# The gate's dot products on GpSimd and ScalarE instead of a column of q's matmuls, and another order of one group of products

## The chip, the cores and the metric

The kernel runs on one core of a Trainium2 chip. A core has five engines that work side by side, each through its own queue and in order: TensorE (PE in the profile, its weight loads PEld), VectorE (DVE), ScalarE (ACT), GpSimd (POOL) and the queue of SyncE (SP), which here only issues transfers. They wait for each other through semaphores. The metric is the device time of one execution in microseconds (us), the median of several runs.

## The reference

Input x has 2048 rows of 448. The output mixes two branches by a gate per row:

```python
g = sigmoid((x * gate_w).sum(-1, keepdims=True))
q, k, v = ...(x @ wqkv)                     # 16 heads of 28
phi = lambda t: where(t > 0, t + 1, exp(t)) + 1e-6
kv = einsum("bhsd,bhse->bhde", phi(k), v); z = phi(k).sum over s
a = (phi(q) @ kv) / (phi(q) @ z + 1e-6) @ wo     # linear attention, no mask
b = causal convolution of x with a kernel made of 256 modes per channel, + x * D_skip
out = g * a + (1 - g) * b
```

With the inputs of this case the convolution's modes allow a short form, which the kernel checks at its end (a general path that follows only if the check fails takes no part here): each channel's b is a running sum of x down the rows, scaled, plus x * D_skip.

## The kernel before

Rows are cut into 16 chunks of 128 (a chunk holds every 16th row, so that the running sum inside a chunk's partition goes over chunks). All large products are 128 x 128 by 128 x 448 on TensorE; to keep their precision each operand is split into a high and a low part, and each product of chunk and weights becomes 11 matmuls (four high by high, four low by high, three high by low; low parts of the small last slice of the weights share a tile with its high part).

The work stands in four stretches.

- **Start** (to 22 us): loads, the split of the first chunks and of the weights, k of chunks 0 to 2, q of chunks 0 and 1.
- **The loop** `for c in range(2, NC - 2)` (L518 on, 22 to 102 us). Step c does on TensorE: k of chunk c + 1 (11 matmuls, `project`, L340, tile `k` or `v`), q of chunk c (11 matmuls, tile `q`), and `do_g(c)`, the sum of phi(k) by x of chunk c (11 matmuls into `g`, L416). v is never formed: x weighted by phi(k) is summed first and multiplied by the weights of v afterwards.
- **Joining** (102 to 120 us): k and q of the last chunks, z summed over the partitions (`zo`, then `zb`), the gate's end (`gate`, L400 to L402), the heads' matrices times wo (`m`), and `norm_a`, `norm_b`, `norm_c`, which divide phi(q) by its dot product with z.
- **Output** (120 to 163 us): `turn_pe` transposes the normed phi(q), `attend` (L677) takes 11 products per chunk, `final_b` (L682) adds (1 - g) * b and stores.

What the other engines do in step c of the loop: ScalarE copies x of chunk c + 2 to the high parts (`split_t`, the transposed x, L241, tile `xt`; `split_n`, the plain x, L247, tile `xn`) and GpSimd takes the low parts (L237). `k_feature(c + 1)` is two activations of ScalarE (L367, L368) and one of VectorE (L369), `k_high` is ScalarE's (L373), `k_low` VectorE's (two instructions of L379, one of which adds to `zb`). `q_post(c)` reads q's PSUM tile on ScalarE and, last, on VectorE (L360 in steps 2 to 4, L394 later). GpSimd also forms x * D_skip (`skip`, L253). In steps 2 to 5 pieces of the filter's preparation (`steps`, L289 to L320) stand in between on ScalarE and VectorE.

The order on each engine is the order in which the code calls these functions; no scheduler moves anything (`manual_schedule`). Until step 5 `split_n(c + 2)` stands at the step's end; from step 6 on it stands at the front, right behind `split_t`:

```python
        split_t(c + 2)
        ...
        if c > 5:
            split_n(c + 2, False)
        k_feature(c + 1, ko)
        ...
        if c < 6:
            split_n(c + 2, c > 3)
```

The tile `q` in PSUM has one buffer, so q of chunk c + 1 waits until `q_post(c)` has read it; k alternates between `k` and other tiles from step 7 on, and chunks 6, 7 and 8 follow each other in `k`. The loads of x (`load_x`, four buffers) wait in SP's queue until a buffer's last reader is done.

The gate: `gate_w` is a 449th column of q's weights (with one of padding, 450 columns), so q's matmuls give x . gate_w in column 448 of q's tile, and `q_post` takes exp(-s) of it on ScalarE (L387, 128x1) into `e1`. `gate(0, c + 1)` with c = 14 (called at L713) makes 1 + e1 and its reciprocal for the first 15 chunks; chunk 15 has its own in `late`.

Of the kernel before, what the change touches and what calls it, by code (L numbers as in the profile page):

```python
# [33 lines left out]
EDGE = 16  # L34
PADS = 32
G = 4
ROWS = {6: (0, 1), 7: (2, 3, 4), 8: (5, 6, 7), 9: (8, 9, 10), 10: (11, 12, 13), 11: (14, 15)}
SMALL = 2.0 ** -70
FLAT = 2.0 ** 35
# [102 lines left out]
@with_exitstack  # L142
def gated_mix_kernel(ctx: ExitStack, tc: tile.TileContext, xin, wq_d, wvo_d, abc_d, ldt_d, dsk_d,
                     turn_d, cst_d, first_d, gin_d, out):
# [24 lines left out]
    ones = const.tile([P, P], F32R, name="ones")  # L169
    dsk = const.tile([P, D], F32, name="dsk")  # L170
    side = []
# [54 lines left out]
    for j in range(0, J, 2):  # L226
        SP.dma_start(out=wqr[:, j:j + 2], in_=wq_d[:, j:j + 2])
    SP.dma_start(out=dsk, in_=dsk_d.to_broadcast([P, D]))
    load_x(3)
# [14 lines left out]
    def split_n(c, both=True):  # L244
        r, w = plain[c], xn_p.tile([P, NX], F32R, name="xn", tag="n")
        xn[c] = w
        ACT.copy(w[:, :XC - NAT], r)  # L247
        if c > 2 and both:
            skip(c)
        low(POOL, w[:, XC - NAT:], r[:, :D], w[:, :D])  # L250

    def skip(c):
        POOL.tensor_tensor(out=y[:, c], in0=plain[c][:, :D], in1=dsk, op=ALU.mult)  # L253

    idle = ps.tile([P, 512], F32, name="q", tag="q")
# [65 lines left out]

    def pieces(c, wh, wl, n, tag, last=None):
        o = ps.tile([P, 512], F32, name=tag, tag=tag)
        h, l = ([xt[c][:, i + k * P:i + (k + 1) * P] for k in range(J)] for i in (0, NAT))
        hh, lh, hl = ([(a[k], w[:, k]) for k in range(J)] for a, w in ((h, wh), (l, wh), (h, wl)))
        hl = hl[1:]
        if last == "x":
            seq = hh + hl + lh
        else:
            seq = [p for k in range(J) for p in (hh[k], lh[k])] + hl  # L330
            if last and len(last) > 1:
                seq = [{"h": hh, "l": lh, "w": [None] + hl}[i[0]][int(i[1])] for i in last.split()]
            elif last == "w":
                seq = seq[2:6] + seq[8:9] + seq[6:8] + seq[9:] + seq[:2]

        def run(count):
            for _ in range(min(count, len(seq))):
                a, b = seq.pop(0)
                run.n += 1
                PE.matmul(o[:, :n], lhsT=a, rhs=b, start=run.n == 1, stop=not seq)  # L340
        run.n = 0
        return o, run
# [43 lines left out]
    def q_post(c, o, mid=None):  # L386
        ACT.activation(e1[:, c:c + 1], o[:, D:D + 1], AF.Exp, scale=-1.0)  # L387
        if c < 5 or c >= NC - 2:
# [129 lines left out]
    for c in range(2, NC - 2):  # L518
# [24 lines left out]
        if c > 5:  # L543
            split_n(c + 2, False)
        k_feature(c + 1, ko)
        if c in (8, 9, 11):
# [7 lines left out]
        if rows:  # L554
            running(rows.pop(0))
        qo = project(c, wqh, wql, D + 2, "q")
        q_post(c, qo)
# [20 lines left out]
        if c in (3, 4):  # L578
            half_load(0, c - 3)
        for j in {11: (0, 1), 12: (2, 3)}.get(c, ()):  # L580
            split_o(j)
# [82 lines left out]
    def attend(c, cuts):  # L664
# [3 lines left out]
        for i, (lo, hi) in enumerate(cuts):  # L668
# [42 lines left out]
    norm_a(0)  # L711
    norm_a(1)
    gate(0, c + 1)  # L713
    norm_bd(0)
# [187 lines left out]
def _layout(inputs):  # L902
# [16 lines left out]
    def tiles(w):  # L919
# [33 lines left out]
        f(byd(inputs["B_log_dt"])[:, :, 0]),  # L953
        f(np.asarray(inputs["B_D_skip"]).reshape(1, D)),
        f(np.stack([np.eye(P), lag >= 1], axis=1)),
# [20 lines left out]
```

## Time and profile before

| | |
|---|---|
| median of 3 runs | 167.91 us (167.91 to 168.14) |
| the profiled execution | 167.58 us |
| its span, first to last instruction | 165.6 us |
| busy: TensorE, VectorE, ScalarE, GpSimd | 97%, 70%, 66%, 63% |

The profiled execution's time is longer than its span, as what lies ahead of the first and behind the last instruction counts in it. A group row reads: line, engine, operation, out<-in, shapes, count, then busy us and mean ns of one, then the engine's idle time just before and what ended it. A timeline row reads: start in us from the span's start, us taken, engine, line, operation, tiles, and in brackets the idle time before it with its releaser. A row of the chain reads start, us, what. A row of a list of waits reads: who waited for whom, us in total, times, longest.

### The profile page before, as it was taken

What the parts mean: (1) busy time and instruction counts of PE and PEld (TensorE: products, weight loads), DVE (VectorE), ACT (ScalarE), POOL (GpSimd) and SP (SyncE); (2) the same over time, 40 slices, a digit from 0 to 9 for tenths busy, and PEclk for the clock granted to TensorE, in tenths of its full rate; (3) what the DMA queues carried; (4) which work ended last, traced back from release to release, by engine and by line L of the source; (5) the groups of instructions that cost most, each with busy time, mean ns of one, the idle gap of its engine ahead of it and who ended that gap; (6) DMA issues with size and microseconds to landing.
All of it is one profiled execution on the core that took longest, in us unless ns stands there. A gap on an engine that the chain in (4) does not pass through costs nothing.

```text
span 165.6 us, 2610 instructions
## 1 busy us (share of the span) xinstructions
PE 160.5 (97%) x835; PEld 144.8 (87%) x835; DVE 116.0 (70%) x243; ACT 109.4 (66%) x257; POOL 104.9 (63%) x116
## 2 busy tenths in 40 slices
PE   6999999999999999999999999999999999999991
PEld 2698999999999999999999999989879999999990
DVE  0937744685852888989885555898899989986441
ACT  3688668898486784776758966453775775666531
POOL 3082589568819439467295999749799998632000
PEclk9999999999999999999999999999999999999999
DMA  5989956597974331969968007998121221122222
GB/s 167 410 311 320 311 156 216 209 316 280 311 260 137 127 107 48 194 156 259 337 200 166 0 4 118 184 204 163 25 49 55 111 111 59 66 103 111 111 85 89
DMA packets 10783, 27.51 MB, mean 166 GB/s; under 512 B 1328, under 2 KB 6992, under 8 KB 10544
## 3 DMA queue, kind: packets, MB, share of 16 engines
q1 hardware_dynamic: 8992, 21.71, 38.3%
q0 software_dynamic: 1632, 5.51, 17.8%
q8 instruction: 7, 0.11, 0.3%
q10 hardware_dynamic: 144, 0.11, 0.2%
q14 instruction: 8, 0.07, 0.1%
HBM read 17.87 MB, written 3.67 MB: 130 GB/s over the span
## 4 chain that ended last, share of the span: by engine, by line
PE 93%; DVE 2%; DMA 1%; ACT 1%; SPq 0%; issue 0%; ACTq 0%; POOL 0%; POOLq 0%
PE g L416 21%; PE a L677 21%; PE q L340 19%; PE v L340 12%; PE k L340 11%; PE tr L633 3%; PE q L259 3%; DMA wk<-shl 1%; PE k L756 1%; SPq L795 0%; ACT kvh L773 0%; DVE wk L744 0%; DVE shl L744 0%; POOL warm L193 0%; DVE ot L682 0%
## 5 line engine op out<-in xcount | busy, mean ns | idle before, releaser
L677 PE MATMUL a<-wk,th 128*128 128x448 f32 (+1 forms) x178 | 37.6, 357 | 0.2 <-DMA wk<-shl 0.2
L416 PE MATMUL g<-pkh,xn 128*128 128x448 f32 x112 | 35.7, 364 | 0.0
L677 PEld LDWEIGHTS a<-wk,th 128*128 128x128 f32 x178 | 31.4, 188 | 2.9 <-issue 0.5
L237 POOL TENSOR_TENSOR xt<-xr,xt 128x512 fp32r<-128x512 f32 x14 | 18.1, 1294 | 19.6 <-ACT xt L241 19.6
L340 PE MATMUL q<-wqh,xt 128*128 128x450 f32 x120 | 27.7, 366 | 0.0
L237 POOL TENSOR_TENSOR xn<-xr,xn 128x448 fp32r<-128x448 f32 x16 | 19.6, 1225 | 9.9 <-ACT xn L247 9.9
L340 PEld LDWEIGHTS q<-wqh,xt 128*128 128x128 f32 x120 | 22.5, 188 | 1.7
L416 PE MATMUL g<-pkl,xn 128*128 128x448 f32 x64 | 23.3, 365 | 0.0
L416 PEld LDWEIGHTS g<-pkh,xn 128*128 128x128 f32 x112 | 21.1, 188 | 2.3
L596 POOL TENSOR_TENSOR prod<-pq,zb 128x448 f32<-128x448 f32 x16 | 18.2, 1149 | 3.9 <-ACT zb L710 2.9
L253 POOL TENSOR_TENSOR y<-xr,dsk 128x448 f32<-128x448 f32 x16 | 20.4, 1280 | 0.0
L340 PE MATMUL k<-wk,xt 128*128 128x448 f32 x88 | 19.7, 366 | 0.0
L340 PE MATMUL v<-wk,xt 128*128 128x448 f32 x88 | 18.9, 362 | 0.0
L340 PEld LDWEIGHTS k<-wk,xt 128*128 128x128 f32 x88 | 16.3, 188 | 1.7 <-DVE xt L237 0.3
L340 PEld LDWEIGHTS v<-wk,xt 128*128 128x128 f32 x88 | 16.5, 188 | 1.1
L682 DVE SCALAR_TENSOR_TENSOR ot<-y,og,a 128x448 f32<-128x448 f32 (+1 forms) x17 | 10.6, 629 | 7.2 <-PE a L677 7.1
L621 POOL TENSOR_TENSOR room<-pq,den 128x336 f32<-128x336 f32 x16 | 12.0, 750 | 5.7 <-ACT den L610 2.7
L688 ACT COPY pq<-a 128x448 f32<-128x448 f32 (+1 forms) x17 | 8.6, 511 | 5.8 <-DVE ot L682 5.6
L416 PEld LDWEIGHTS g<-pkl,xn 128*128 128x128 f32 x64 | 11.1, 174 | 1.1 <-DVE pkl L379 0.2
L340 PE MATMUL q<-wql,xt 128*128 128x450 f32 x45 | 11.7, 365 | 0.0
L655 ACT CAST th<-tr 64x128 fp32r<-64x128 f32 x32 | 8.3, 260 | 4.9 <-DVE th L646 4.5
L369 DVE SCALAR_TENSOR_TENSOR k<-k,e 128x448 f32<-128x448 f32 x8 | 5.0, 631 | 8.9 <-ACT e L368 8.8
(155 smaller groups left out, 288.9 us busy)
## 6 DMA issues: line engine op xcount, KB each, us to landing
xr<-in SPq DMA_DIRECT2D x15, 512.0 KB, 4.6
out<-ot SPq DMA_DIRECT2D x15, 224.0 KB, 1.9
room<-in SPq DMA_DIRECT2D x3, 896.0 KB, 8.0
wvo<-in SPq DMA_DIRECT2D x2, 896.0 KB, 5.6
y<-wvo POOLq DMA_DIRECT2D x2, 896.0 KB, 7.7
y<-room POOLq DMA_DIRECT2D x2, 896.0 KB, 9.2
y<-over POOLq DMA_DIRECT2D x2, 896.0 KB, 9.5
y<-in SPq DMA_DIRECT2D x2, 480.0 KB, 4.3
```

Source lines behind the costliest of these rows:

```text
L237: eng.tensor_tensor(out=o, in0=r, in1=h.bitcast(F32), op=ALU.subtract)
L253: POOL.tensor_tensor(out=y[:, c], in0=plain[c][:, :D], in1=dsk, op=ALU.mult)
L259: PE.matmul(idle[:, :cols], lhsT=warm[:, :P], rhs=warm[:, :cols], start=True, stop=True)
L340: PE.matmul(o[:, :n], lhsT=a, rhs=b, start=run.n == 1, stop=not seq)
L369: DVE.scalar_tensor_tensor(out=pks[c], in0=pks[c], scalar=1.0, in1=e, op0=ALU.add, op1=ALU.max)
L416: PE.matmul(g[i][:a.shape[1], :D], lhsT=a, rhs=b, start=c == 0 and n == 0, stop=c == NC - 1 and n == len(seq) - 1)
L596: POOL.tensor_tensor(out=pd[c], in0=pq[:, c], in1=zb, op=ALU.mult)
L621: POOL.tensor_tensor(out=n[:, :3, :DJ].rearrange("p j (h d) -> p j h d", h=4), in0=a, in1=r[:, :H - 4].rearrange("p (j h) -> p j h", j=3)[ ...
L655: ACT.copy((th, tl)[i][c][half, 3], oe[i * DT:(i + 1) * DT, 3 * P:])
L677: PE.matmul(a[:, lo:hi], lhsT=u_, rhs=w_[:, lo:hi], start=n == 0, stop=n == 10)
L682: DVE.scalar_tensor_tensor(out=ot[:, lo:hi], in0=y[:, c, lo:hi], scalar=og[:, c:c + 1], in1=a[:, lo:hi], op0=ALU.mult, op1=ALU.add)
L688: ACT.copy(pq[:, c, lo:hi], a[:, lo:hi])
```

## The change

For chunks 2 to 13 the gate's dot product leaves TensorE. GpSimd multiplies plain x by gate_w, broadcast to all partitions (`gate_products`, into the three buffers of `prod`, which `norm_a` uses later), and ScalarE adds up each row with an accumulating copy (`gate_total`, into `e1`). One exponential over the twelve columns of `e1` follows in the joining stretch, ahead of `gate`. q's matmuls of these chunks have 448 columns instead of 450, and `q_post` has no exponential for them. Chunks 0, 1, 14 and 15 keep the column. D_skip and gate_w come in one broadcast load of two rows. `PADS` grows by 64 columns, so that the tiles behind keep their alignment. The table `GATES` says which chunks' products stand at the end of step c; their sums stand in step c + 1, between the copies of x and `k_feature`. Apart from that, the nine products of the first output chunk stand in another order.

```diff
+GATES = {2: (2,), 3: (3,), 4: (4, 5, 6), **{c: (c + 2,) for c in range(5, 12)}}
...
-    dsk = const.tile([P, D], F32, name="dsk")
+    both_rows = const.tile([P, 2, D], F32, name="rows")
+    dsk, gwt = both_rows[:, 0], both_rows[:, 1]
...
-    SP.dma_start(out=dsk, in_=dsk_d.to_broadcast([P, D]))
+    SP.dma_start(out=both_rows, in_=rows_d.to_broadcast([P, 2, D]))
...
+    def gate_products(c):
+        POOL.tensor_tensor(out=prod[:, c % 3], in0=plain[c][:, :D], in1=gwt, op=ALU.mult)
+
+    def gate_total(c):
+        ACT.activation(prod[:, c % 3], prod[:, c % 3], AF.Copy, accum_out=e1[:, c:c + 1])
...
     def pieces(c, wh, wl, n, tag, last=None):
+        wh, wl = wh[:, :, :n], wl[:, :, :n]
...
     def q_post(c, o, mid=None):
-        ACT.activation(e1[:, c:c + 1], o[:, D:D + 1], AF.Exp, scale=-1.0)
+        if c < 2 or c >= NC - 2:
+            ACT.activation(e1[:, c:c + 1], o[:, D:D + 1], AF.Exp, scale=-1.0)
...
         if c > 5:
             split_n(c + 2, False)
+        for i in GATES.get(c - 1, ()):
+            gate_total(i)
         k_feature(c + 1, ko)
...
-        qo = project(c, wqh, wql, D + 2, "q")
+        qo = project(c, wqh, wql, D, "q")
...
         if c in (3, 4):
             half_load(0, c - 3)
+        for i in GATES.get(c, ()):
+            gate_products(i)
...
             if c == 0:
-                seq = [seq[n] for n in (0, 2, 3, 6, 1, 4, 5, 7, 8)]
+                seq = [seq[n] for n in (0, 2, 1, 3, 4, 5, 6, 7, 8)]
...
     norm_a(1)
+    ACT.activation(e1[:, 2:c], e1[:, 2:c], AF.Exp, scale=-1.0)
     gate(0, c + 1)
```

The order on GpSimd from the end of step 2 to step 5, before (`xn` and `xt` are the low parts of x, `y` is x * D_skip; in brackets the semaphores an instruction waits for):

```order
L237 TENSOR_TENSOR xn<-xr,xn 128x448 [waits Activation_49]
L237 TENSOR_TENSOR xt<-xr,xt 128x512 [waits DVE_49,DMAHW6_49,PE_49,Activation_49]
L253 TENSOR_TENSOR y<-xr,dsk 128x448
L253 TENSOR_TENSOR y<-xr,dsk 128x448 [waits DVE_49]
L237 TENSOR_TENSOR xn<-xr,xn 128x448 [waits Activation_49,Pool_49]
L237 TENSOR_TENSOR xt<-xr,xt 128x512 [waits DMAHW0_49,PE_49,Activation_49]
L253 TENSOR_TENSOR y<-xr,dsk 128x448 [waits Pool_49]
L237 TENSOR_TENSOR xn<-xr,xn 128x448 [waits Activation_49]
L237 TENSOR_TENSOR xt<-xr,xt 128x512 [waits DMAHW2_49,PE_49,Activation_49]
```

The same place in the change:

```order
L239 TENSOR_TENSOR xn<-xr,xn 128x448 [waits Activation_49]
L258 TENSOR_TENSOR prod<-xr,rows 128x448
L239 TENSOR_TENSOR xt<-xr,xt 128x512 [waits DVE_49,DMAHW6_49,PE_49,Activation_49]
L255 TENSOR_TENSOR y<-xr,rows 128x448
L255 TENSOR_TENSOR y<-xr,rows 128x448 [waits DVE_49]
L239 TENSOR_TENSOR xn<-xr,xn 128x448 [waits Activation_49,Pool_49]
L258 TENSOR_TENSOR prod<-xr,rows 128x448
L239 TENSOR_TENSOR xt<-xr,xt 128x512 [waits DMAHW0_49,PE_49,Activation_49]
L255 TENSOR_TENSOR y<-xr,rows 128x448 [waits Pool_49]
L239 TENSOR_TENSOR xn<-xr,xn 128x448 [waits Activation_49]
L258 TENSOR_TENSOR prod<-xr,rows 128x448 x3
L239 TENSOR_TENSOR xt<-xr,xt 128x512 [waits PE_49,DMAHW2_49,Activation_49,Pool_49]
```

Each product of the gate (`prod`) stands right behind the low part of xn, which itself waits for ScalarE's copy, and ahead of the low part of the next xt.

The order on ScalarE in step 3, before (`e<-k` is L367, the start of k's feature; `sums<-q` is the first reading of q's tile, with the exponential of the gate's column just ahead of it; `y,sm` are the filter's preparation):

```order
L247 CAST xn<-xr 128x512
L241 CAST xt<-xr 128x512 [waits DMAHW6_49]
L367 ACTIVATE e<-k 128x448 [waits PE_49]
L368 ACTIVATE e<-e 128x448 [waits Activation_49]
L373 ACTIVATE pkh<-k 128x448 [waits DVE_49]
L387 ACTIVATE e_61<-q 128x1 [waits PE_49]
L356 ACTIVATE sums<-q 128x448
L294 ACTIVATE y,sm<-pq 112x512
```

The same place in the change:

```order
L249 CAST xn<-xr 128x512
L243 CAST xt<-xr 128x512 [waits DMAHW6_49]
L261 ACTIVATE prod,e_61<-prod 128x448 [waits Pool_49]
L376 ACTIVATE e<-k 128x448 [waits PE_49]
L377 ACTIVATE e<-e 128x448 [waits Activation_49]
L382 ACTIVATE pkh<-k 128x448 [waits DVE_49]
L365 ACTIVATE sums<-q 128x448 [waits PE_49]
L302 ACTIVATE y,sm<-pq 112x512
```

The sum of chunk 2's products (`prod,e_61`) stands ahead of k's feature and waits for GpSimd; the exponential of one column is gone.

The products of the first output chunk on TensorE, before, from the first product on (the DMA semaphores tell of the rows of `mh`, part of `wk`, that transfers bring; VectorE's tell of low parts):

```order
L677 MATMUL a<-wk_70,th 128x448 [waits DMAHW3_49,DVE_49,Activation_49]
L677 MATMUL a<-wk_70,th 128x448 [waits DVE_49]
L677 MATMUL a<-wk_70,th 128x448 [waits DMAHW4_49,Activation_49]
L677 MATMUL a<-wk_70,th 128x448 [waits DMAHW5_49,Activation_49]
L677 MATMUL a<-wk_70,th 128x448 [waits DVE_49]
```

The same in the change:

```order
L691 MATMUL a<-wk_70,th 128x448 [waits DMAHW3_49,DVE_49,Activation_49]
L691 MATMUL a<-wk_70,th 128x448 [waits DVE_49] x2
L691 MATMUL a<-wk_70,th 128x448 [waits DMAHW4_49,Activation_49]
L691 MATMUL a<-wk_70,th 128x448
L691 MATMUL a<-wk_70,th 128x448 [waits DVE_49]
L691 MATMUL a<-wk_70,th 128x448 [waits DMAHW5_49,Activation_49]
```

The wait for the third of these transfers (DMAHW5) moved from the fourth product to the seventh, and one for VectorE came ahead, to the third.

More of the change, by code (lines that the diff above doesn't have):

```diff
@@ L34 @@
 EDGE = 16
-PADS = 32
+PADS = 96
 G = 4
 ROWS = {6: (0, 1), 7: (2, 3, 4), 8: (5, 6, 7), 9: (8, 9, 10), 10: (11, 12, 13), 11: (14, 15)}
+GATES = {2: (2,), 3: (3,), 4: (4, 5, 6), **{c: (c + 2,) for c in range(5, 12)}}
 SMALL = 2.0 ** -70
@@ L142, in gated_mix_kernel @@
 @with_exitstack
-def gated_mix_kernel(ctx: ExitStack, tc: tile.TileContext, xin, wq_d, wvo_d, abc_d, ldt_d, dsk_d,
+def gated_mix_kernel(ctx: ExitStack, tc: tile.TileContext, xin, wq_d, wvo_d, abc_d, ldt_d, rows_d,
                      turn_d, cst_d, first_d, gin_d, out):
@@ L953, in _layout @@
         f(byd(inputs["B_log_dt"])[:, :, 0]),
-        f(np.asarray(inputs["B_D_skip"]).reshape(1, D)),
+        f(np.stack([np.asarray(inputs["B_D_skip"]).reshape(D), np.asarray(inputs["gate_w"]).reshape(D)[perm]])[None]),
         f(np.stack([np.eye(P), lag >= 1], axis=1)),
```

## The prediction

> **What bounds the kernel now.** I read the page's busy shares first, then TensorE's waits, then the chain in order of time, then the timelines of ScalarE, GpSimd and VectorE in the stretch where the change first acts.
>
> ```profile
> span 165.6 us, 2610 instructions
> PE 160.5 (97%) x835; PEld 144.8 (87%) x835; DVE 116.0 (70%) x243; ACT 109.4 (66%) x257; POOL 104.9 (63%) x116
> PE a L677 <- DMA wk<-shl: 0.2, 1, 0.2
> ```
>
> TensorE is busy for 97% of the span, and beside the wait for its first operand its list of waits has this one entry. So the time is its stream of products, and only two things change it: fewer or shorter products, or a wait that does not exist today. The 66% of ScalarE and the 63% of GpSimd look like room, but they are averages. This is the stretch of chunks 3 and 4 (columns: window, sum, then busy us of PE, PEld, DVE, ACT, POOL, each with its count; then clock and DMA):
>
> ```profile
> 28.00:35.00 7.00, 7.00 (x37) 6.41 (x36) 4.96 (x11) 6.17 (x18) 5.34 (x6) 1.00 0.69 239
> ```
>
> ScalarE is busy for 6.17 of 7.00 us there, because the filter's preparation is interleaved with chunks 2 to 4. A wait in its queue has almost nothing to swallow it, and the change puts one there.
>
> **The new wait, step by step.** At the end of loop step c GpSimd computes xn's low part (L237), and then, new, the gate's products. In step c+1 ScalarE copies xt, then, new, sums those products, and only then starts k's feature (L367). Both engines take their work in order. Today's rows, ScalarE first (start, length):
>
> ```profile
> 31.57 0.53 ACT L367 ACTIVATE e<-k 128x448 f32<-128x448 f32 x1
> 34.36 0.63 ACT L294 ACTIVATE y<-pq 112x512 f32<-112x512 f32 x1
> 36.41 0.42 ACT L295 ACTIVATE y<-room 112x256 f32<-112x256 f32 x1
> 36.83 0.60 ACT L247 CAST xn<-xr 128x512 fp32r<-128x512 f32 x1
> 37.86 0.53 ACT L367 ACTIVATE e<-v 128x448 f32<-128x448 f32 x1
> 40.83 0.63 ACT L247 CAST xn<-xr 128x512 fp32r<-128x512 f32 x1
> 43.83 0.55 ACT L367 ACTIVATE e<-k 128x448 f32<-128x448 f32 x1 [1.85 <-PE k L340]
> 45.98 0.55 ACT L373 ACTIVATE pkh<-k 128x448 fp32r<-128x448 f32 x1 [0.99 <-DVE k L369]
> 48.56 0.62 ACT L247 CAST xn<-xr 128x512 fp32r<-128x512 f32 x1
> 50.85 0.55 ACT L367 ACTIVATE e<-k 128x448 f32<-128x448 f32 x1 [0.63 <-PE k L340]
> ```
>
> GpSimd's rows; the one of L253 is the same product (128x448, two SBUF operands) that the gate now takes, and it prices it: 1.15 us, the next starting 0.04 before it ends, so 1.12 each in a row.
>
> ```profile
> 31.22 1.24 POOL L237 TENSOR_TENSOR xn<-xr,xn 128x448 fp32r<-128x448 f32 x1 [1.66 <-ACT xn L247]
> 37.57 1.18 POOL L237 TENSOR_TENSOR xn<-xr,xn 128x448 fp32r<-128x448 f32 x1 [1.62 <-ACT xn L247]
> 39.97 1.15 POOL L253 TENSOR_TENSOR y<-xr,dsk 128x448 f32<-128x448 f32 x1
> 41.54 1.16 POOL L237 TENSOR_TENSOR xn<-xr,xn 128x448 fp32r<-128x448 f32 x1 [0.42 <-ACT xn L247]
> ```
>
> A sum over 448 elements isn't in the trace; it lies between the 0.42 us of 256 elements (L295) and the 0.63 of 512 (L294), and I take 0.57, by length. What it removes, the exponential of one column, moves its successor by only 0.05 us. Now the ring, with delays of L367 against today:
>
> - Chunk 2. GpSimd ends xn at 31.22 + 1.24 = 32.46 and the product at 33.58; ScalarE's sum starts at 33.61 and L367 of chunk 4 at 34.18 instead of 31.57: 2.6 us late.
> - Chunk 3. From that L367 to the end of the next xn copy ScalarE needs 37.43 - 31.57 - 0.05 = 5.8 us and so ends it at 39.99; GpSimd starts 0.14 later, takes 1.18 and 1.12, and the sum ends at 43.0 instead of 37.86: 5.2 late.
> - Chunks 4, 5 and 6, three products at once. The copy ends 3.55 us on, at 46.6; then 0.08 + 1.16 + 3 x 1.12, and the last sum ends at 51.8 instead of 43.83: 7.95 late. The idle 1.85 us of ScalarE before 43.83 is used up in this.
> - Chunk 7. To the next xn copy (48.56 + 0.62) it was 5.35, less 0.05 and less 0.29 (L373 waited 0.99 for VectorE, of which 0.29 was a backlog that has passed by then): 56.8; then 0.08 + 1.16 + 1.12 + 0.6: 59.7 instead of 50.85, 8.9 late.
> - Chunk 8 on. From step 6 xn is split before k's feature and not at the step's end, so the product is one step old when it is asked for: no further wait.
>
> What is late next is TensorE, because q and k each reuse a PSUM buffer that VectorE must have read out:
>
> ```profile
> 36.95 1.81 PE L340 MATMUL q<-wqh,xt 128*128 128x450 f32 x8
> 43.63 1.77 PE L340 MATMUL q<-wqh,xt 128*128 128x450 f32 x8
> 48.45 2.36 PE L340 MATMUL k<-wk,xt 128*128 128x448 f32 x11
> 55.06 2.36 PE L340 MATMUL k<-wk,xt 128*128 128x448 f32 x11
> 35.78 0.62 DVE L360 SCALAR_TENSOR_TENSOR pq<-q,t 128x448 f32<-128x448 f32 x1
> 42.06 0.62 DVE L360 SCALAR_TENSOR_TENSOR pq<-q,t 128x448 f32<-128x448 f32 x1
> 47.10 0.61 DVE L379 SCALAR_TENSOR_TENSOR zb<-k,zb 128x448 f32<-128x448 f32 x1
> 53.82 0.61 DVE L379 SCALAR_TENSOR_TENSOR pkl<-k,pkh 128x448 fp32r<-128x448 f32 x1
> ```
>
> q of chunk 4 starts at 36.95 and its buffer is free at 36.40, 0.55 us of room; 2.6 late it waits about 2.1. q of chunk 5 (43.63, free at 42.68 + 5.15) waits another 2.1 to 2.2, k of chunk 7 (48.45, free at 47.71 + 7.65) 2.6, k of chunk 8 (55.06, free at 54.43 + 8.9 and a tenth for the start) 1.4. After that TensorE is **8.3 us** late and nothing gives it back, as it has no idle time later. Bounds: the sum at 0.42 or 0.63 moves this by 0.5 down or 0.2 up over four rings; a product at the 1.28 us that L253 has as its mean adds 0.8.
>
> **What the other parts give.** In order of time, TensorE alone:
>
> ```profile
> 37.11 2.27 PE q L340 x11
> 43.79 2.21 PE q L340 x11
> 41.59 2.20 PE k L340 x11
> ```
>
> Eleven products of 450 columns take 2.21 or, in five groups of fourteen, 2.27 us; of 448 columns they take 2.20. Gains before 55 us vanish into the waits; behind it chunks 7, 9 and 11 had the 2.27 (with 0.01 on the products behind each): 0.27 us with the rest. Bounds: 0.05 and 0.3.
>
> The first output chunk: its products start at 120.14, and the copies of the rows of mh land one after the other:
>
> ```profile
> 120.14 1.06 PE L677 MATMUL a<-wk,th 128*128 128x448 f32 x3
> 121.39 1.85 PE L677 MATMUL a<-wk,th 128*128 128x448 f32 x8 [0.20 <-DMA wk<-shl]
> 119.95 0.67 DVE L646 TENSOR_TENSOR th<-tr,th 128x512 fp32r<-128x512 f32 x1
> ```
>
> Today the fourth product needs the third of four copies (it starts at 121.39, as soon as that has landed), and it is the first of the last eight. In the new order it is the seventh; the third needs VectorE's low part of th (119.95 + 0.67 = 120.62) and starts near 120.73, the fourth near 121.0, the seventh near 121.6, and the last ends its issue near 122.6 instead of 123.1: 0.48 us. VectorE is nearly as busy as TensorE behind this, so part is taken by its waits: I take 0.3, bounds 0 and 0.48.
>
> The gate itself: its exponential now stands behind ScalarE's zb copy.
>
> ```profile
> 109.26 0.53 ACT L710 COPY zb<-zo 128x448 f32<-128x448 f32 x1 [0.73 <-PE zo L708]
> 109.64 0.17 DVE L400 TENSOR_SCALAR e<-e 128x15 f32<-128x15 f32 x1
> 110.12 1.01 DVE L402 TENSOR_SCALAR og<-og 128x15 f32<-128x15 f32 x1
> 109.94 2.27 POOL L596 TENSOR_TENSOR prod<-pq,zb 128x448 f32<-128x448 f32 x2 [2.90 <-ACT zb L710]
> 114.12 0.28 DVE L762 TENSOR_TENSOR k<-k,mask 112x112 f32<-112x112 f32 x1
> ```
>
> L402 took 1.01 us where its like L400 took 0.17: it ended when GpSimd's first product of the two did (109.94 + half of 2.27). L400 can now start at about 109.9, in a race with that product. Ahead of it, the gate ends 0.1 later; behind it, L400 ends with the first product and L402 with the second, 1.1 us later, and L762, which starts 114.12 and is on the chain, follows. I take 0.05, bounds 0 and 1.1. [...]
>
> The broadcast load is 224 KB larger and stands ahead of x of chunk 3 in SP's queue:
>
> ```profile
> xr<-in SPq DMA_DIRECT2D x15, 512.0 KB, 4.6
> L241 ACT CAST xt<-xr 128x512 fp32r<-128x512 f32 x14 | 8.6, 613 | 0.3 <-DMA xr<-in 0.3
> ```
>
> At 512 KB in 4.6 us it makes that x at most 2.0 us later. ScalarE's fourteen copies of x wait for loads for 0.3 us in all, and chunk 3's comes behind the work on chunks 0 to 2, so I take nothing, bounds 0 and 2.0. The later loads of x wait for a buffer whose last reader may now be a gate product; they land a step or more ahead of their use, so I count nothing there either.
>
> Sum: 8.3 - 0.27 - 0.3 + 0.05 = **7.8 us**. The profiled execution took 167.58 us (165.6 of span and 1.98 around it) and would take 175.4; the median is 167.91, so **175.7**.
>
> **Rivals.** (1) The sums never hold ScalarE, because the products are done in time: then only the gains stay, 0.35 + 0.3 less 0.05, and the time is 167.3, faster. For it speak GpSimd's 1.6 us idle before each xn; against it, that this idle lies before the xn copy, on which the product waits in line. (2) The wait comes, but something I count as serial overlaps (the ring closes once, at chunk 2 and 3, and the idle of ScalarE at 43.83 absorbs the rest): 2.1 + 2.1 - 0.6, so 171.5. Against it: three products in a row at chunk 4. (3) TensorE slows after the stalls. At the start ten products of 512 columns took 3.85 us:
>
> ```profile
> 1.33 3.85 PE q L259 x10
> ```
>
> At the later pace (448 columns in 0.20) they would take 2.3. After each stall but the last the ring, not TensorE, sets the next start, so one such loss counts: 1.6 us, 177.3. [...] (4) L400 loses its race: 176.8. (5) The 448 columns don't shorten anything, since the 2.27 comes from elsewhere: 176.0.
>
> **How the numbers follow.** Forecast with (4) and (5) as its edges 0.75, (3) 0.06, (2) 0.09, (1) 0.07, and 0.03 for an even balance. The range 172.5 to 178.2 takes in the price bounds (0.5 down, 0.2 and 0.8 up), (3), (4), and a wait that closes in one ring less. About 0.2% is what a measurement of this kernel can tell from no change: faster by more 0.07, within 0.03, slower 0.90.
>
> **What would show it.** Right: TensorE's list of waits gets VectorE as releaser, with two waits of about 2.1 us at q and two of 2.6 and 1.4 at k, between 38 and 64 us; ScalarE idles about 1.9 us before the sums of chunks 2, 3 and 4, released by GpSimd; q's eleven products take 2.20 from chunk 7 on; from step 8 to the loop's end TensorE waits for nothing; the first output chunk's products have no wait over 0.3. Wrong: TensorE's waits stay under 2 us in sum (rival 1), or its products take longer than 0.20 after a wait (rival 3), or the gate's last step ends over 2 us behind the zb copy (1.3 today; rival 4).

## The result, and the profile after

On the chip the changed kernel takes 175.81 us (median of five runs, 175.17 to 175.87), the one before 167.91 on the same chip (167.87 to 168.23): a ratio of 1.0445, 95% interval 1.0421 to 1.0469. The profiled execution took 175.17, with a span of 173.4 instead of 165.6, so 7.8 us more. The page after:

```profile
span 173.4 us, 2622 instructions
PE 163.0 (94%) x835; PEld 145.5 (84%) x835; DVE 115.7 (67%) x243; ACT 116.0 (67%) x270; POOL 118.1 (68%) x128
PEclk9999999999969999999999999999999999999999
```

TensorE's share fell from 97% to 94%, and the row of its clock, 40 slices of the span, has a dip in the twelfth slice that the page before did not have. Its list of waits now has VectorE as releaser:

```profile
PE q L349 <- DVE pq L369: 3.7, 2, 1.8
PE k L349 <- DVE pkl L388: 1.1, 1, 1.1
PE k L349 <- DVE zb L388: 0.9, 1, 0.9
```

In time these are four starts. The rows answer to the four of L340 in the prediction:

```profile
39.06 1.88 PE L349 MATMUL q<-wqh,xt 128*128 128x448 f32 x8 [1.83 <-DVE pq L369]
...
47.89 2.62 PE L349 MATMUL q<-wqh,xt 128*128 128x448 f32 x8 [1.83 <-DVE pq L369]
...
55.46 2.45 PE L349 MATMUL k<-wk,xt 128*128 128x448 f32 x11 [0.88 <-DVE zb L388]
...
63.46 2.45 PE L349 MATMUL k<-wk,xt 128*128 128x448 f32 x11 [1.14 <-DVE pkl L388]
```

Before they started at 36.95, 43.63, 48.45 and 55.06: TensorE is 2.11, 4.26, 7.01 and 8.40 us late, of which 0.1 stood already at the start of the loop. (The idle time in brackets counts from the modelled end of the product before, 0.37 us behind its start, so it is about 0.17 less than what is lost at 0.20 us a product.) Where VectorE's input stays away is read on ScalarE:

```profile
33.67 0.58 ACT L261 ACTIVATE prod<-prod 128x448 f32<-128x448 f32 x1 [1.93 <-POOL prod L258]
...
34.24 0.53 ACT L376 ACTIVATE e<-k 128x448 f32<-128x448 f32 x1
...
42.49 0.58 ACT L261 ACTIVATE prod<-prod 128x448 f32<-128x448 f32 x1 [1.93 <-POOL prod L258]
...
43.07 0.53 ACT L376 ACTIVATE e<-v 128x448 f32<-128x448 f32 x1
...
48.96 0.58 ACT L261 ACTIVATE prod<-prod 128x448 f32<-128x448 f32 x1 [1.83 <-POOL prod L258]
...
51.74 0.52 ACT L376 ACTIVATE e<-k 128x448 f32<-128x448 f32 x1
...
59.16 0.58 ACT L261 ACTIVATE prod<-prod 128x448 f32<-128x448 f32 x1 [1.40 <-POOL prod L258]
...
59.74 0.53 ACT L376 ACTIVATE e<-k 128x448 f32<-128x448 f32 x1
```

L376 (L367 before) started at 31.57, 37.86, 43.83 and 50.85. It is 2.67, 5.21, 7.91 and 8.89 us late; the prediction had 2.6, 5.2, 7.95 and 8.9.

Two things in this trace were not forecast. Behind the second wait TensorE's products come 0.373 us apart instead of 0.20 (the row at 47.89 takes 2.62 us for eight products, the one at 39.06 takes 1.88). And the first output group is no shorter than before:

```profile
128.23 3.12 PE L691 MATMUL a<-wk,th 128*128 128x448 f32 x11
131.19 0.93 PE L647 MATMUL tr<-both,room 128*128 128x128 f32 x7
```

From its first product to the next transposes it takes 2.96 us; before it was 2.94 (120.14 to 123.08).

### The profile page after: what moved, and what is told of

It reads as the page before. It is cut to its first block, busy times and chain, and to the rows that moved or that the text cites. A ratio compares the mean times of both kernels' runs of the same rounds, so it can differ in the third digit from the quotient of the medians.

```text
span 173.4 us, 2622 instructions
## 1 busy us (share of the span) xinstructions
PE 163.0 (94%) x835; PEld 145.5 (84%) x835; DVE 115.7 (67%) x243; ACT 116.0 (67%) x270; POOL 118.1 (68%) x128
## 4 chain that ended last, share of the span: by engine, by line
PE 61%; ACT 2%; DVE 1%; issue 1%; ACTq 0%
PE a L691 21%; PE q L349 11%; PE g L426 11%; PE k L349 5%; PE v L349 5%; PE tr L647 4%; PE m L751 1%; PE tr L771 1%; PE k L771 1%; ACT prod L261 0%; DVE k L378 0%; DVE pkl L388 0%; ACT e L377 0%; ACT pkh L382 0%; DVE ot L696 0%
## 5 line engine op out<-in xcount | busy, mean ns | idle before, releaser
L349 PE MATMUL q<-wqh,xt 128*128 128x448 f32 (+1 forms) x120 | 28.4, 373 | 3.7 <-DVE pq L369 3.7
L255 POOL TENSOR_TENSOR y<-xr,rows 128x448 f32<-128x448 f32 x16 | 20.3, 1277 | 0.0
L258 POOL TENSOR_TENSOR prod<-xr,rows 128x448 f32<-128x448 f32 x12 | 14.5, 1214 | 0.0
L261 ACT ACTIVATE prod<-prod 128x448 f32<-128x448 f32 x12 | 6.9, 577 | 8.0 <-POOL prod L258 8.0
L349 PE MATMUL q<-wql,xt 128*128 128x448 f32 (+1 forms) x45 | 12.2, 377 | 0.0
```

The source lines that it names most:

```text
L258: POOL.tensor_tensor(out=prod[:, c % 3], in0=plain[c][:, :D], in1=gwt, op=ALU.mult)
L261: ACT.activation(prod[:, c % 3], prod[:, c % 3], AF.Copy, accum_out=e1[:, c:c + 1])
```

## The experiments

Each run is compared with runs of the kernel before on its own chip; the medians of the kernel before were 167.92, 167.78 and 168.28 us on the three chips used. Besides the time this table gives four stretches of the profiled execution, all on TensorE, in us: from the first product of chunk 5's k to that of chunk 8's (the ring lies in it), from there to the first output product, the first output group, and the rest of the span (to 0.05 us, as the page gives spans to 0.1).

| kernel | ratio to before, 95% | ring | to output | first group | rest |
|---|---|---|---|---|---|
| before | 1 | 20.31 | 65.08 | 2.94 | 42.52 |
| the change | 1.0445 (1.0421 to 1.0469) | 28.62 | 64.77 | 2.96 | 42.21 |
| sums behind `k_high` | 1.0135 (1.0089 to 1.0182) | 22.57 | 65.08 | 3.07 | 42.26 |
| sums of a resident row | 1.0109 (1.008 to 1.0139) | 22.62 | 64.68 | 2.98 | 42.37 |
| products without sums | 1.0031 (1.0011 to 1.005) | 21.79 | 64.65 | 2.97 | 42.19 |
| chunk 2 alone | 1.0151 (1.0085 to 1.0217) | 24.06 | 65.08 | 2.49 | 42.56 |
| chunk 2 alone, again | 1.0141 (1.0103 to 1.0179) | 22.50 | 65.13 | 2.44 | 42.80 |
| chunk 2 three times | 1.044 (1.0421 to 1.0458) | 27.83 | 64.96 | 2.45 | 42.79 |
| old order of products | 1.0478 (1.0441 to 1.0516) | 28.62 | 64.75 | 4.29 | 42.42 |
| twelve fills | 1.0449 (1.0425 to 1.0474) | 28.62 | 64.74 | 2.47 | 42.42 |
| before, new order | 0.9972 (0.9959 to 0.9985) | 20.31 | 65.09 | 2.48 | 42.52 |
| before, 448 columns | 1.001 (0.9997 to 1.0024) | 20.23 | 64.78 | 3.60 | 42.82 |
| chunks 4 to 13 | 0.9988 (0.9957 to 1.002) | 20.53 | 64.75 | 2.47 | 42.32 |
| chunks 6 to 13 | 0.9938 (0.9921 to 0.9954) | 20.31 | 64.88 | 2.48 | 42.18 |

### Is it the wait for GpSimd, or the work?

The sums moved, nothing else:

```diff
-        for i in GATES.get(c - 1, ()):
-            gate_total(i)
         k_feature(c + 1, ko)
...
         k_high(c + 1)
+        for i in GATES.get(c - 1, ()):
+            gate_total(i)
         k_low(c + 1)
```

> The changed kernel, but each gate sum on ScalarE stands behind k_high(c + 1) and not ahead of k_feature(c + 1); all products and sums are kept. Theory (the loss is the wait in ScalarE's queue, a ring of two queues): the products are done when the sums are asked for, k's feature is late only by the sums' own 0.57 us each, TensorE waits for 0.4 us at most between 36 and 66 us, and the time is 167.3 to 167.9 us. Rival (the loss is the work: 6.9 us more on ScalarE and 14.5 on GpSimd, in a stretch where ScalarE is busy for 88%): the same work in another place still holds TensorE by several us, 171 to 175.

Measured: 170.36 us (169.58 to 171.71), a ring of 22.57 instead of 28.62. So 6 of the 8.3 us were the wait for GpSimd. But 2.3 remained where I had expected 0.4, and it was no rest of that wait. On ScalarE:

```profile
39.33 0.62 ACT L243 CAST xt<-xr 128x512 fp32r<-128x512 f32 x1 [1.35 <-DMA xr<-in]
```

and by groups, in the same kernel:

```profile
L243 ACT CAST xt<-xr 128x512 fp32r<-128x512 f32 x14 | 8.6, 613 | 2.4 <-DMA xr<-in 2.4
```

ScalarE's copies of x wait for their loads for 2.4 us in all. The kernel before has the same group with 0.3. This is another wait, one that the prediction had put at nothing.

The sums left in their place, but without anything to wait for:

```diff
-        ACT.activation(prod[:, c % 3], prod[:, c % 3], AF.Copy, accum_out=e1[:, c:c + 1])
+        ACT.activation(junk, dsk, AF.Copy, accum_out=e1[:, c:c + 1])
```

> The changed kernel with the sums in their place ahead of k_feature, but summing the resident row D_skip instead of the products, into a tile of their own: the 0.57 us of ScalarE and the 1.15 of GpSimd stay, only the wait for GpSimd is gone (the gate of chunks 2 to 13 is left out by this, so the output is another). Theory (wait): k's feature of chunk 4 is 0.5 us late, of chunk 5 1.0, q of chunk 5 waits 0.1 to 0.2, and ScalarE's idle 1.85 us before k's feature of chunk 6 takes the rest; 167.3 to 167.9. Rival (work): TensorE waits for 3 us and more, over 170.

Measured: 169.99 us (169.46 to 170.48), ring 22.62. Its copies of x wait for loads too, 1.9 us in the groups of that kernel. Neither text was right: without the wait for GpSimd 6 us go, and 2.3 stay.

The products alone:

```diff
-        for i in GATES.get(c - 1, ()):
-            gate_total(i)
```

> The changed kernel without the gate's sums (their columns of e1 are filled with zero, so the gate of chunks 2 to 13 is left out); the products stay where they are. Theory (the products alone hold the buffers of x: x of chunk 6 goes out at 36 us behind the second x * D_skip instead of at 26, lands at 39.3, and ScalarE's copy of it, due at 37.3, waits for about 2 us): k's feature of chunk 5 is 2.0 late, q of chunk 5 has 0.95 us of room and waits 1.0, k of chunk 7 0.3 to 0.5; 168.4 us. Rival (the products cost nothing where no sum waits for them): no wait over 0.2, 167.2.

Measured: 168.49 us (168.18 to 169.21), ring 21.79. ScalarE has no work of the gate's here, and yet:

```profile
39.65 0.62 ACT L244 CAST xt<-xr 128x512 fp32r<-128x512 f32 x1 [1.99 <-DMA xr<-in]
```

It waits 2.0 us for x of chunk 6, as expected. q of chunk 5 then comes 1.1 late and k of chunk 7 0.2. The products hold a buffer of x, and without any sum this costs 1.5 us in the ring's stretch. The 0.8 between this kernel and the two before comes with the sums; how it divides between their own time on ScalarE and what waits behind them was not measured. In the changed kernel the late load is there too. SP sends it off at 36.03, and ScalarE's copy of it starts at 39.95 without a wait:

```profile
36.03 0.33 SPq L204 DMA_DIRECT2D xr<-in  x1
...
39.95 0.62 ACT L243 CAST xt<-xr 128x512 fp32r<-128x512 f32 x1
```

In the kernel before, this second load of the loop went off at 26.10:

```profile
26.10 0.33 SPq L202 DMA_DIRECT2D xr<-in  x1
```

Then it took the buffer of chunk 3, whose last reader (its xn low part) ended at 26.07. Now chunk 3's gate product at the end of step 3 still reads that buffer, and the load waits for the one that the first `skip` of step 3 frees, at 36.0. It lands at 39.37, so that ScalarE's copy, delayed by the ring, starts 0.58 us later. The ring hid the late load.

### Does TensorE give anything back, and when does it slow down?

One gate product instead of twelve:

```diff
-GATES = {2: (2,), 3: (3,), 4: (4, 5, 6), **{c: (c + 2,) for c in range(5, 12)}}
+GATES = {2: (2,)}
...
-        qo = project(c, wqh, wql, D, "q")
+        qo = project(c, wqh, wql, D if c == 2 else D + 2, "q")
```

(with the exponential of the column kept for the other chunks)

> The changed kernel with the gate of chunk 2 alone on GpSimd and ScalarE; chunks 3 to 13 keep their column and their exponential. Theory (what TensorE loses once stays lost): q of chunk 4 waits 2.1 us; the next features are late by no more than TensorE is, so no second wait; 167.9 + 2.1 = 170.0, between 169.5 and 170.3. Rival (ScalarE's idle 1.85 us before k's feature of chunk 6 gives it back): 167.9 to 168.3. As to TensorE's pace: if a single idle time of 2 us slows it, the products behind it take 0.37 us instead of 0.20 for about 3 us and the time is 171.6; if it takes two such waits within 10 us, as in the changed kernel, they stay at 0.20.

Measured: 170.68 us, four executions from 169.79 to 172.24. One wait, at q of chunk 4, and none behind it. In the profiled execution (171.02 us) the products behind the wait came 0.37 us apart; by windows (window, length, busy us of PE, PEld, DVE, ACT, POOL with counts, then clock, DMA share and GB/s):

```profile
36.27:39.69 3.42, 1.50 (x9) 1.09 (x8) 2.93 (x7) 3.32 (x12) 0.81 (x1) 1.00 0.79 307
39.69:43.10 3.41, 3.41 (x11) 3.02 (x10) 1.52 (x4) 2.45 (x5) 2.90 (x3) 0.50 0.08 25
```

The clock was 0.50 for one stretch of 3.41 us: its row counts 11 products, where a row of the same length at 1.00 counts 19 (41.94:45.35 of the next run). Nothing behind hid it, so the ring's stretch grew by 3.75 us: 2.15 of wait and 1.6 of slow products. So here slow products followed a single wait, of 2.15 us, which the expectation had left open. But other executions were faster, so I ran it again.

> The gate of chunk 2 alone once more, for the spread: one wait of 2.1 us at q of chunk 4, nothing behind it that hides slower products. The first time the profiled execution had products of 0.37 us for 3.4 us behind the wait, took 171.0 and showed a mean granted clock of 0.990; two others took 169.8 and 170.3 with 1.00. Theory (whether the clock falls behind a wait of 2 us differs from one execution to the next, as if the wait were measured against a grid of its own): executions near 169.5 (167.9 + 2.1 - 0.45 for the order of the first output chunk) with a clock of 0.995 and more, and others near 171.1 with 0.99, few between. Rival (a wait of 2 us never slows it and the first profile was a disturbance): all near 169.5. Rival (always): all near 171.1.

Measured: six executions, from the fastest to the slowest, with their mean granted clock: 169.36 (1.00), 169.92 (1.00), 170.09 (1.00), 171.05 (0.990), 171.34 (0.995), 171.49 (0.996). The profiled one (169.92) has the same wait of 2.1 us and no slow product:

```profile
35.11:38.52 3.41, 2.38 (x12) 1.88 (x11) 2.31 (x4) 2.65 (x9) 2.18 (x2) 1.00 1.03 392
38.52:41.94 3.42, 2.53 (x13) 2.39 (x14) 2.00 (x7) 3.27 (x8) 1.52 (x2) 1.00 0.13 54
41.94:45.35 3.41, 3.41 (x19) 3.14 (x18) 2.69 (x5) 2.29 (x6) 2.99 (x3) 1.00 0.74 253
```

So whether the clock falls differs from one execution to the next. The times don't part as cleanly as I wrote: the execution with a clock of 0.990 is 1.0 to 1.7 us above those with 1.00, but two others are as slow with 0.995 and 0.996, where the profiled 171.02 with its 3.41 us at 0.50 has 0.990, and so was the 172.24 of the first run (0.996). What held those three up stays open; no trace shows it.

What decides it is not shown. The traces show these times. In the changed kernel's the clock is recorded as full from 4.41 us on (the warm-up products of 512 columns come 0.427 us apart ahead of it and 0.216 behind it), falls at 48.79, which is 44.37 us or 13 times 3.413 later, and rises again at 52.20, after 3.413. In the one of the kernel before it is up from 4.68 to 165.11, which is 160.43 us or 47 times 3.413. With chunk 2 alone, with the twelve fills and with chunk 2 three times the clock is 0.50 in a window of 3.41 or 3.42 us (39.69:43.10, 40.20:43.62, 43.88:47.29). Both long stretches are whole multiples of the 3.413 us for which the clock stayed low, and the windows above are cut in steps of it; whether such steps run on through every execution, two traces don't settle. Products fill 1.50 of 3.42 us in the window ahead of the fall, but 2.38 and 2.53 in the two that the same wait was spread over in the second run. That alone does not decide it: the last section has a window with 1.59 us of products and no fall behind it.

A longer wait:

```diff
-GATES = {2: (2,)}
+GATES = {2: (2, 2, 2)}
```

> As the run before, with chunk 2's product and sum done three times (the same values each time), so that the one wait is longer: GpSimd 2.24 us later, ScalarE 1.1, k's feature of chunk 4 5.9 late, q of chunk 4 waits 5.4. Theory: behind a wait of this length the clock falls in every execution, 0.37 us a product for about 3.4 us, 1.6 us more: 167.9 + 5.4 + 1.6 - 0.45 = 174.4. Rival (a longer wait makes no difference to what one of 2 us does): a mixture of 172.9 and 174.4.

Measured: 175.55 us (175.08 to 175.96), against 168.28 for the kernel before on this chip. The wait came in two pieces, because the low part of xt that v needs stood behind the products on GpSimd:

```profile
37.68 2.27 PE L349 MATMUL v<-wk,xt 128*128 128x448 f32 x10 [2.04 <-POOL xt L239]
...
43.38 1.04 PE L349 MATMUL q<-wqh,xt 128*128 128x450 f32 x3 [3.42 <-DVE pq L369]
```

TensorE lost 7.52 us in the ring's stretch: 5.9 of waiting and 1.6 of slow products. All four executions have a clock of 0.99 or less (0.99, 0.99, 0.99, 0.971), as the theory has it. "Every execution" is not shown by four.

### The first output group: what the new order is worth

The kernel before with the new order alone:

```diff
-                seq = [seq[n] for n in (0, 2, 3, 6, 1, 4, 5, 7, 8)]
+                seq = [seq[n] for n in (0, 2, 1, 3, 4, 5, 6, 7, 8)]
```

> The kernel before with only the new order of the first output chunk's products. Theory: with the copies landing 0.62 us apart the new order has no wait for the third copy, the group takes 2.49 instead of 2.94 us, and since VectorE's waits behind it take little, the time is 167.5 (0.4 less). Rival (VectorE is the bound behind this place and takes it back): 167.9.

Measured: 167.44 us (167.15 to 167.81) against 167.78, ratio 0.9972 (0.9959 to 0.9985). The group takes 2.48 us, and the rest of the span is 42.52 as before: VectorE takes nothing back. So the order is worth 0.46 us in the group and 0.34 in the medians. And the changed kernel with the order of before:

```diff
-                seq = [seq[n] for n in (0, 2, 1, 3, 4, 5, 6, 7, 8)]
+                seq = [seq[n] for n in (0, 2, 3, 6, 1, 4, 5, 7, 8)]
```

> The changed kernel with the products of the first output chunk in the order of before. In the changed kernel's trace the third transfer of mh's rows landed 1.74 us behind the first of these products, in the one of before 1.12. Theory A (the late landing is there with either order, and the new one hides it): the fourth product waits for it, the group takes 0.5 us more, 176.3 us. Theory B (the landing is as in before, and the new order gains nothing): within 0.2 of 175.8. Theory C (the new order gains 0.3 to 0.48 as forecast, lost elsewhere): 176.1 to 176.3, with the third landing 1.1 to 1.2 behind the first product. The ring is unchanged: waits of 2.0, 2.0, 1.0 and 1.3, and if the slow products (0.37 us each) behind the second wait belong to the ring and not to that one execution, they are there again.

Measured: 176.22 us (176.14 to 176.82), with a group of 4.29 us:

```profile
129.12 0.44 PE L691 MATMUL a<-wk,th 128*128 128x448 f32 x1 [0.30 <-DMA wk<-shl]
130.09 1.46 PE L691 MATMUL a<-wk,th 128*128 128x448 f32 x6 [0.53 <-DMA wk<-shl]
132.00 0.64 PE L691 MATMUL a<-wk,th 128*128 128x448 f32 x2 [0.45 <-DMA wk<-shl]
```

Theory A holds: TensorE waits for three of the four copies. The group is 1.33 us longer than the changed kernel's, more than the theory said, but part of this belongs to that execution, the slowest of the six: its last copy took 4.1 us from issue to landing, where the other profiles have 2.2 to 2.5. The kernel with the columns alone (below), which has the old order and late copies too but not this one, takes 3.60, and the ratios to before (1.0478 and 1.0445) differ by 0.55 us. So the new order does gain about 0.6 us in the changed kernel. It is spent at once on copies that come late. In the kernel before the copies landed 0.62 to 0.68 us apart; in the changed kernel the second and third came 0.94 and 0.96 us behind the one before them. Why? In its transfers between 125.70 and 130.20 there is one packet that the same stretch of the kernel before does not have:

```profile
q14 instruction: 1, 0.01, 0.4%
wk<-shl SPq DMA_DIRECT2D x3, 56.0 KB, 2.5
```

The profile lists it as instruction, so I take it for a fetch of instructions. It comes at 128.4 us, and the copies' median from issue to landing is 2.5 us instead of 2.2. Before, the fetch nearest to this came at 115.5, ahead of the copies. In both kernels it comes when VectorE is at its 187th or 188th recorded instruction (counting also those that only wait for a semaphore); that it fetches VectorE's is my estimate from these two counts, as no row names the engine. VectorE's queue has 61 such waiting instructions before and 49 after: one fewer for each chunk that lost its gate column (60 with chunk 2 alone, 53 and 51 where eight and ten chunks lost it). If the fetch is VectorE's, twelve instructions fewer ahead of it move it twelve instructions later, and that is among the copies. To test it I put twelve instructions back that do nothing:

```diff
+    pad = const.tile([P, 64], F32, name="pad")
+    for i in range(12):
+        DVE.memset(pad[:, i:i + 1], 0.0)
```

> The changed kernel with twelve tiny fills (128x1, into a tile of their own) at the head of VectorE's queue, where VectorE waits for its first load. Why: without the gate's column VectorE's queue has 12 waiting instructions fewer, and in the four kernels without the column the fetch of instructions that comes near VectorE's 187th instruction falls between the four copies of mh's rows (128.4 us in the changed kernel; 115.5 before, ahead of them). Theory (that fetch holds up the copies): it is ahead of the copies again, they land 0.6 us apart as before and not 0.95, the first output group takes 2.49 us instead of 2.96, and the time is 175.3. Rival (the copies land late for another cause, such as the shifted additions of GpSimd's transfers): 2.96 as in the changed kernel, 175.8. The ring's waits (2.0, 2.0, 1.0, 1.3) stay.

Measured: a group of 2.47 us, the fetch at 123.8, no such packet among the copies, and from issue to landing

```profile
wk<-shl SPq DMA_DIRECT2D x3, 56.0 KB, 2.2
```

So with the fetch moved ahead of them the copies were on time; how one packet of 0.01 MB goes with two copies that are 0.3 us late each is not shown. In the time little of it arrives: 175.29 us (175.19 to 175.73), the ratio to before is the same as the changed kernel's, since the start and the rest of the span were each 0.2 longer in this profile. The expectation's 175.3 was met, but on another chip than the 175.81, so I don't count it as a gain that was measured.

The columns alone, with the kernel before's order:

```diff
-        qo = project(c, wqh, wql, D + 2, "q")
+        qo = project(c, wqh, wql, D, "q")
```

(the exponential reads another column)

> The kernel before with q of chunks 2 to 13 in 448 columns (the gate's exponential reads another column, so the gate of these chunks is left out); nothing else is changed. Theory: the five groups of eleven products that took 2.27 us take 2.20, 0.07 each and 0.01 on the group behind each, 0.35 to 0.45 in all; 167.5. Rival (the 2.27 comes from elsewhere): 167.9.

Measured: 168.43 us (168.16 to 168.89) against 168.28: nothing gained. But the trace shows the gain and what ate it. From the first product of chunk 2's q to the first output product TensorE took 96.03 us instead of 96.43, so 0.40 less, as expected. Then this, with the same packet q14 in the copies' stretch:

```profile
120.92 0.45 PE L679 MATMUL a<-wk,th 128*128 128x448 f32 x1 [0.30 <-DMA wk<-shl]
121.89 1.85 PE L679 MATMUL a<-wk,th 128*128 128x448 f32 x8 [0.52 <-DMA wk<-shl]
```

The first output group takes 3.60 us, 0.66 more. Here too VectorE has twelve waiting instructions fewer, and the fetch comes at 120.2 us. Six kernels without the twelve have the fetch between the copies and a median of 2.4 or 2.5 us to landing; the others have no fetch there and 2.2.

### A version without the waits

Gates for fewer chunks, each product behind its own xn low part (so that a buffer of x is held for one product longer, not for two steps), the sums behind `k_high`, and fills for the waiting instructions that went:

```diff
-GATES = {2: (2,), 3: (3,), 4: (4, 5, 6), **{c: (c + 2,) for c in range(5, 12)}}
+GATES = {c: (c + 2,) for c in range(4, 12)}
...
-        qo = project(c, wqh, wql, D, "q")
+        qo = project(c, wqh, wql, D if c >= 6 else D + 2, "q")
...
+    for i in range(8):
+        DVE.memset(pad[:, i:i + 1], 0.0)
```

(and the sums moved as in the first experiment; this is the version for chunks 6 to 13, the one for 4 to 13 has `range(2, 12)`, `c >= 4` and ten fills)

> The gate on GpSimd and ScalarE for chunks 4 to 13 alone: the products of chunk c + 2 stand behind its own xn low part at the end of step c (so a buffer of x is held 1.1 us longer and not two steps longer), the sums stand behind k_high, chunks 0 to 3, 14 and 15 keep the column, ten tiny fills at the head of VectorE's queue. Theory (two waits: GpSimd's products, and behind them the loads of x, which the products of chunks 3 and 4 sent out 10 us late): both are gone, ScalarE's copies of x wait for loads for under 0.3 us in sum, TensorE for 0.3 at most, the first output group takes 2.49; 167.9 - 0.45 - 0.3 + 0.3 = 167.4. Rival (the sums' own 0.57 us in ScalarE's tight stretch, chunks 4 and 5): TensorE still waits 1 us and more before 50 us; 168.3 to 169.

Measured, chunks 4 to 13: 167.19 us (166.72 to 168.86), ratio 0.9988 (0.9957 to 1.002). TensorE's list of waits has none in the loop; ScalarE's copies wait 0.2 us for loads, and the second load of the loop goes off at 26.15 again. The ring's stretch is 0.22 longer than before, from the first two products of chunk 6's k, 0.29 late. So both waits are gone, as the theory has it, and in this place the sums' own time costs no more than this. The profiled execution took 166.72, but four of twelve took 168.65 to 168.86, with clocks of 0.996 to 1.00 and for a cause that no trace shows, and no gain can be told from the median.

> As the run before, but for chunks 6 to 13 alone and with eight fills: no sum stands in ScalarE's tight stretch (28 to 42 us). Theory: no wait of TensorE at all between 22 and 100 us, the groups of 2.27 us in chunks 7, 9 and 11 become 2.20 (0.27 with what follows them), the first output group takes 2.49 (0.45): 167.9 - 0.7 = 167.2. Rival (the sums and products cost wherever they stand): 168.5 and more.

Measured, chunks 6 to 13: 166.82 us (166.70 to 167.12) against 167.78, ratio 0.9938 (0.9921 to 0.9954): 1.0 us faster than before, and by the two ratios 5% faster than the change. The kernel before with the new order alone took 167.44 on the same chip, so 0.6 us of this comes with the gate. Its list of waits has one entry, the first operand at the start:

```profile
PE q L270 <- POOL warm L195: 1.3, 1, 1.3
```

## Why the prediction was right, point by point

The forecast was 175.7 us, the result 175.81.

**The ring** (forecast 8.3 us): right in size and place. The four delays of k's feature are within 0.07 us of the worked-out ones (0.1 of each was there from the start), the sum takes 0.58 us (taken: 0.57), the products follow each other by 1.1, and TensorE lost 8.31 us in the ring's stretch and waited for nothing from there to the loop's end. That the wait is the cause, and not the work, was shown by moving the sums: 6 of the 8.3 us go with that.

**"So I count nothing there either"** (the later loads of x): wrong. The step failed on "they land a step or more ahead of their use". The load of chunk 6's x goes off 10 us later, because a buffer is held by a gate product two steps on. It cost nothing in the changed kernel only because the ring was later still, by 0.58 us. The products alone cost 1.5 us in the ring's stretch through it, and they are most of the 2.3 that stay with the sums moved. The total was right although this term was wrong, and a repair of the ring alone would have been priced 2 us too well, as the expectation for the moved sums shows (0.4 us of waits, 2.3 measured).

**TensorE's pace behind the waits** (rival 3): the mechanism came, the price did not. Products of more than 0.20 us behind a wait were named as a sign that the prediction is wrong, and on this point it was: the clock did fall, to 0.50, behind waits listed with 1.8 us at most:

```profile
45.37:48.79 3.42, 1.59 (x8) 1.15 (x7) 3.10 (x10) 1.76 (x5) 2.10 (x2) 1.00 0.72 258
48.79:52.20 3.41, 3.41 (x11) 3.01 (x11) 1.49 (x10) 2.37 (x7) 3.41 (x4) 0.50 0.57 172
```

It fell behind the second wait, and 1.6 us of slow products were hidden: TensorE then waited 1.0 us at chunk 7's k instead of 2.6, because the ring sets that start, as the rival's text had it for all stalls but the last. In the profile with the twelve fills the clock fell behind the first wait instead, and the ring's stretch is 28.62 us in both. Two of the five executions of the changed kernel have a mean clock of 0.977 and 0.978, twice the loss, and took no longer for it (175.87 and 175.81 us, against 175.17 to 175.82 with 0.99). Had the clock fallen behind the last wait, nothing would have hidden it, as nothing did with chunk 2 alone. The forecast has no term for this loss; that it came out right all the same depends on where the clock fell.

**448 columns** (-0.27): right. From chunk 8's k to the first output product it is 0.31 less, and alone in the kernel before 0.40 over the whole loop.

**The first output chunk's order** (-0.3 of a computed 0.48): mis-sized. The 0.48 was right where the copies land on time (0.46 measured, nothing taken back by VectorE). In the changed kernel the group is 0.02 longer than before, because the change itself made the copies late; the prediction's term did not see the fetch. The 0.3 us that the sum needs came from elsewhere: the rest of the span is 42.21 instead of 42.52. That stretch varies from 42.18 to 42.82 among these profiles without a cause that I can name, so this term came out by luck.

**The gate** (+0.05, rival 4): right in size.

```profile
118.14 2.31 POOL L610 TENSOR_TENSOR prod<-pq,zb 128x448 f32<-128x448 f32 x2 [2.88 <-ACT e L727]
...
118.14 0.17 DVE L410 TENSOR_SCALAR e<-e 128x15 f32<-128x15 f32 x1 [0.23 <-ACT e L727]
...
118.64 0.72 DVE L412 TENSOR_SCALAR og<-og 128x15 f32<-128x15 f32 x1
```

The race was a tie, which the prediction didn't have: GpSimd's product and L410 started at the same 118.14, and L410 was not held, it takes 0.17 as before. L412 ends at 119.36, about when the first of GpSimd's two products does and 1.36 us behind the zb copy (1.34 before), and L777 follows without a wait that is put down to it.

**The broadcast load** (0): no copy of x waits for it in the changed kernel (0.1 us in all fourteen).

## What to carry to other kernels

Follow a new instruction along three lines: what queues behind it on its own engine, what it waits for, and which buffer it holds; the third gave a 2 us wait that the first one hid. When a wait is removed, look in the trace for what was due just behind it (here a load that landed 0.58 us before its use) ahead of pricing the repair. Look also at what a saving moves: here twelve waiting instructions of VectorE fewer went with a fetch at 128.4 us instead of 115.5, among the copies that TensorE needs next.

## What the runs showed of the hardware

- Behind waits of TensorE its clock was 0.50 for 3.41 us in some executions, with products 0.373 us apart instead of 0.20. Products fill 1.59 us of the window ahead of the fall in the changed kernel and 1.50 with chunk 2 alone (rows above); with the twelve fills, at the first wait, and with chunk 2 three times it is

```profile
36.79:40.20 3.41, 1.58 (x9) 1.14 (x8) 3.27 (x7) 3.32 (x12) 0.54 (x1) 1.00 0.85 274
40.20:43.62 3.42, 3.42 (x11) 3.07 (x10) 0.34 (x2) 1.55 (x5) 3.25 (x3) 0.50 0.40 151
...
40.46:43.88 3.42, 0.50 (x3) 0.50 (x4) 2.92 (x7) 3.32 (x12) 0.00 (x0) 1.00 0.24 97
43.88:47.29 3.41, 3.41 (x11) 3.03 (x10) 1.52 (x4) 2.45 (x5) 2.96 (x3) 0.50 0.20 42
```

  and around the third wait of the kernel with the twelve fills the clock stayed up:

```profile
50.44:53.86 3.42, 2.71 (x16) 2.10 (x14) 0.88 (x4) 2.24 (x7) 3.25 (x3) 1.00 0.79 283
53.86:57.27 3.41, 1.59 (x8) 1.53 (x9) 1.78 (x3) 3.35 (x7) 0.19 (x1) 1.00 1.02 384
57.27:60.68 3.41, 3.41 (x19) 3.20 (x18) 0.00 (x0) 1.97 (x6) 3.41 (x4) 1.00 0.97 335
```

  The second of these rows has 1.59 us of products too and no fall behind it, so the rows' busy time does not part the two cases.
- One packet of queue q14 (instruction) lay between the copies of mh's rows in six profiles: the changed kernel, old order, sums behind `k_high`, sums of a resident row, products without sums, and before with 448 columns. There the median of the first three copies from issue to landing was 2.4 or 2.5 us; in the other eight it was 2.2. In the changed kernel the second and third landed 0.94 and 0.96 us behind the one before them, in the kernel before 0.62 and 0.64.
- A sum over 448 elements by an accumulating copy takes 0.58 us on ScalarE, with the start of the accumulator's reading (0.19, from 34.15 in the sum that starts at 33.67) inside it: the next activation starts 0.57 us behind the sum's own start. Behind an activation of 448 elements without a sum the next one starts after 0.47 (36.52 to 36.99 in the changed kernel), so about 0.1 of the reading shows, by this difference.
- In the kernel before, eleven products of 450 columns took 2.21 us in some groups and 2.27 in others, of 448 columns 2.20; why is open.
